# Second buffers for four input tiles, and a two-operation decode of every second weight block, in a fused attention and feed-forward kernel

## The chip, the core and the metric

The kernel runs on one core of one Trainium2 chip. TensorE (PE) multiplies, with its weight loads on a row of their own (PEld); VectorE (DVE), ScalarE (ACT) and GpSimd (POOL) do the elementwise work; SyncE (SP) issues most of the transfers. The metric is the device time of one execution in microseconds, the median of several runs.

## The reference

Causal attention in float32 for 4 batches and 8 heads of 576 rows of 64, blended by a gate per head with a read from a memory matrix; the result goes through a two-layer feed-forward with a sigmoid-approximated GELU.

```python
scores = scale * np.matmul(q, k.transpose(0, 1, 3, 2))
a = softmax(where(causal, -1e9, scores))
local = np.matmul(a, v)
q_p = phi(q)                                   # relu(x) + exp(min(x, 0))
mem_out = (q_p @ M_prev) / (q_p @ z_prev + 1e-6)
x = g * mem_out + (1 - g) * local              # 2304 tokens x 512
h = x @ w_in                                   # 512 x 2048
g = h * (1.0 / (1.0 + np.exp(-1.702 * h)))
out = g @ w_out
```

The weights arrive as float64 values, as pairs of 32-bit words, and are turned into float32 on the chip.

## The kernel before

The program has three stages. A short first part (to about 28 us) does the first 256 query rows of batch 0 for all four head pairs at once. Then sixteen (batch, head pair) units p0 to p15 of attention follow, and the feed-forward's first layer fills TensorE between their steps; from about 385 us on the second layer runs alone.

For one unit the scores are four query blocks (`ps`), 128 to 512 keys wide, and a tail (`ps`, 288 wide). Each block's two heads use the upper and the lower 64 rows of the array: `s_both` writes them as two matmuls one after the other. VectorE takes the row maximum (`nm`, L541), ScalarE the exponential (`a`, `at`, L547), GpSimd scales the rows (L550), TensorE transposes (`pt`), ScalarE and VectorE copy the transposes out (`e`), and TensorE multiplies by the values (`po`). Queries for the memory read go a way of their own: `load_vq` fetches raw queries `qr`, values `vr`, memory `mr` and normaliser `zb`; ScalarE makes exp(min(q, 0)) in `qmin` and `qexp` (tile `qmt`, L489 and L492), VectorE finishes it in `qphi` (`qp`, L496), GpSimd multiplies by `zb`, and so on. The pool `ldp`, which holds `mr`, `qr` and `zb`, has one buffer of each; `kqf` and `vr` have two.

The first layer works on 16 weight blocks (`wi0` to `wi15`). A block is decoded by `conv_unit` in five parts: `load` fetches 128 x 1024 raw words (`wraw`, 512 KB); `scale` has ScalarE rescale the high words into PSUM (`ws`, L213); `bits` are three VectorE operations that shift the result left by 3 (L224), put in the sign from the high word (L229) and put in three bits of the low word (L231, result `wr`); `high` has ScalarE round it to the short form (`wi`, first half); and GpSimd subtracts to get the remainder (second half). TensorE multiplies a block in twelve matmuls (`pm`), the first of which needs only the first half. Decoding takes place up to about 97 us; after that the blocks stay.

What stands before what on each engine is fixed when the program is built: `at(slot, prio, fn)` puts steps into slots, and a scheduler then orders the instructions of each engine by its own estimate of when their inputs and buffers are there. Each engine runs its list strictly in that order, so a change of buffers also moves instructions. Raw words take their buffers from several pools by the letter of the block in a string of sixteen: c is a pool of two, e a pool of two, h and l borrow the tiles of the split activations.

Of the kernel before, what the change touches and what calls it, by code (L numbers as in the profile page):

```python
# [8 lines left out]
F32 = mybir.dt.float32  # L9
F32R = mybir.dt.float32r  # L10
I32 = mybir.dt.int32
AF = mybir.ActivationFunctionType
ALU = mybir.AluOpType
# [21 lines left out]
def tile_attention_memory_moe(ctx, tc, kq, vq, mem, zz, beta, w_in, w_out, out):  # L35
    nc = tc.nc
# [12 lines left out]
    def pool(stack, name, bufs=1, **kw):  # L49
        return stack.enter_context(tc.tile_pool(name=name, bufs=bufs, **kw))  # L50

    attn = ExitStack()
    left = ExitStack()
    cst = pool(ctx, "cst", side="left")
    mop = pool(left, "mop", 2, side="left")
# [7 lines left out]
    ps_m = pool(left, "ps_m", 2, space=PSUM, side="left")  # L63
    dr = pool(ctx, "dr", space=bass.MemoryType.DRAM)
    mox = pool(attn, "mox", 2, side="right")
    ldp = pool(attn, "ldp", side="right")
    att = pool(attn, "att", side="right")
    wkp = pool(attn, "wkp", side="right")
    sml = pool(attn, "sml", 6, side="right")
    ps_s = pool(attn, "ps_s", 4, space=PSUM, side="right")  # L70
    ps_x = pool(attn, "ps_x", 1, space=PSUM, side="right")
    ps_o = pool(attn, "ps_o", 1, space=PSUM, side="right")
# [5 lines left out]
    state = {"slot": -8, "pe": 0.0, "seq": 0, "sum": 0, "bank": 0}  # L78
# [19 lines left out]
    NOSYNC = mybir.DependencyInfo(mybir.DependencyClass.NoSync, mybir.DependencyReason.DATA)  # L98
# [16 lines left out]
    def at(slot, prio, fn):  # L115
        assert slot > state["slot"], (slot, state["slot"])
        state["seq"] += 1
        events.setdefault(slot, []).append((prio, state["seq"], fn))
# [34 lines left out]
    def sub(eng, dst, src, hi):  # L153
        return tt(eng, dst, src, f32(hi), ALU.subtract)
# [7 lines left out]
        out=mask[:, 384:512], in_=mask[:, 384:512], compare_op=ALU.is_ge, fill=NEG,  # L162
# [4 lines left out]
    for r in range(2):  # L167
        v = maskt[64 * r:64 * r + 64, CH - 64:CH]
        nc.gpsimd.affine_select(
            out=v, in_=v, compare_op=ALU.is_ge, fill=NEG, base=0, pattern=[[-1, 64]], channel_multiplier=1)  # L170
# [26 lines left out]

    wb = {}

    def conv_unit(slot, dst, src, rp, rkw, wp, wkw, sp, skw):  # L200
        box = {}

        def load():
            raw = rp.tile([128, DM, 2], I32, name="wraw", **rkw)
            nc.sync.dma_start(raw.rearrange("p f w -> p (f w)"), src.bitcast(I32))
            box["raw"] = raw

        def scale():
            if wp() is None:
                box["s"] = box["r"] = sp.tile([128, DM], F32, name="wr", **skw)  # L210
            else:
                box["s"] = wp().tile([128, DM], F32, name="ws", **wkw)
            x = nc.scalar.activation(  # L213
                out=box["s"], in_=box["raw"][:, :, 1].bitcast(F32), func=AF.Copy, scale=2.0 ** -112)
            for name in (state["behind"], state.get("late A")):
                if name is not None:
                    tc.add_manual_dep(x.ins, name, NOSYNC, reason="raw words")
            state["behind"] = x.ins.name

        def bits():  # L220
            raw, si = box["raw"], box["s"].bitcast(I32)
            if "r" not in box:
                box["r"] = sp.tile([128, DM], F32, name="wr", **skw)
            x = nc.vector.tensor_scalar(out=si, in0=si, scalar1=3, scalar2=None, op0=ALU.logical_shift_left)  # L224
            if "late V" in state:
                tc.add_manual_dep(x.ins, state["late V"], NOSYNC, reason="raw words")
            for name in state.pop("bits", ()):
                tc.add_manual_dep(x.ins, name, NOSYNC, reason="raw words")
            nc.vector.scalar_tensor_tensor(  # L229
                out=si, in0=raw[:, :, 1], scalar=-2 ** 31, in1=si, op0=ALU.bitwise_and, op1=ALU.bitwise_or)  # L230
            nc.vector.scalar_tensor_tensor(  # L231
                out=box["r"].bitcast(I32), in0=raw[:, :, 0], scalar=29, in1=si,
                op0=ALU.logical_shift_right, op1=ALU.bitwise_or)

        def high():
            x = copy("A", dst[:, 0], box["r"])
            if "fqt" in state:
                tc.add_manual_dep(x.ins, state.pop("fqt"), NOSYNC, reason="raw words")

        parts = (load, scale, bits, high,  # L240
                 lambda: sub("P", dst[:, 1], box["r"], dst[:, 0]))
        if slot is None:
            return parts
        for k, prio, fn in zip((0, 2, 2, 3, 3), (5, 60, 61, 40, 41), parts):
            at(slot + k, prio, fn)

# [19 lines left out]
    def conv_in(blk):  # L268
        w = w1[blk].tile([128, 2, DM], F32R, name=f"wi{blk}")
        if blk < AHEAD:  # L270
            wb[blk] = w
        raw = {
            "c": (cnv, {"bufs": 2}), "e": (ear[0], {"tag": "r"}),
            "h": (mop, {"tag": "xh"}), "l": (mop, {"tag": "xl"})}["cceehlcchleeccee"[blk]]
        ws = (lambda: ps_o, {"tag": "po"}) if blk == 3 else (lambda: ps_x, {"tag": "ps"})
        parts = conv_unit(None, w, w_in[blk], *raw, *ws, att, {"tag": f"qpt{blk % 2}", "bufs": 2})
        if blk < AHEAD:
            return parts

        c = CONV[blk - AHEAD]  # L280
        at(max(c - 6, -7), 58, parts[0])
        for fn in parts[1:]:
            at(c, 58, fn)
        at(c + 3, 1, lambda: wb.update({blk: w}))
# [149 lines left out]
    pairs = [(b, c) for b in range(B) for c in range(NP)]  # L434
    raws = {}
# [3 lines left out]
    K0 = [STEP * p for p in range(MB * NP)]  # L439
# [9 lines left out]
            nc.sync.dma_start(kqr, kq[b, c])  # L449
        raws[p] = {"kq": kqr}  # L450

    def load_vq(p):
        b, c = pairs[p]

        vr = att.tile([128, 5, 128], F32, name="vr", bufs=2)
        nc.sync.dma_start(vr, vq[b, c, :, 0])
        mr = ldp.tile([128, 2, D], F32, name="mr")
        nc.sync.dma_start(mr, mem[b * NP + c])
        qr = ldp.tile([128, 5, 128], F32, name="qr")
        t = 2 if b < MB else 0  # L460
        nc.sync.dma_start(qr[:, t:], vq[b, c, :, 1, t:])
        zb = ldp.tile([128, 128], F32, name="zb")
        nc.sync.dma_start(zb, zz[b, c:c + 1, :].to_broadcast([128, 128]))
        raws[p].update(v=vr, m=mr, q=qr, z=zb)


    def hold(p, x):
# [3 lines left out]
    def plan_prep(p):  # L471
        b, c = pairs[p]
        s0 = K0[p] - 8
# [59 lines left out]
        at(s0 + 13, 31, qev)  # L533
        if p + 1 < len(pairs):
            at(K0[p + 1] - 11, 60, lambda: load_kq(p + 1))
            at(max(K0[p + 1] - 8, s0 + 8), 60, lambda: load_vq(p + 1))

    def softmax_max(pieces):
        nm = sml.tile([128, 2], F32, name="nm")
# [263 lines left out]
    for b in range(MB):  # L803
        parts = first_queries(b)
        xplan[b] = -7
        if b == 0:
            for blk in range(AHEAD):
                for fn in (parts[1:] if blk == 0 else conv_in(blk)):
                    fn()
            state["first", 2] = state["behind"]  # L810
    first.close()
    w1.update({k: pool(left, f"w1_{k}", side="left", reuse_waits="tile") for k in range(W0, NB - 2)})
    load_kq(0)
    load_vq(0)
    for p in range(NPAIRS):
        plan_prep(p)
        plan_attend(p)
# [196 lines left out]
    k = 0  # L1014
    while fill["gen"] is not None or conv_q or events:
# [4 lines left out]
        if k in soon:  # L1020
            t, p = soon[k]
# [120 lines left out]
```

## Time and profile before

| | |
|---|---|
| median of 3 runs | 615.9 us (615.55 to 618.78) |
| the profiled execution, its own time | 616.93 us |
| its span, first to last instruction | 615.2 us |
| granted TensorE clock, mean over the span | 0.986 |
| busy: PE 593.0, PEld 518.4, DVE 421.7, ACT 347.9, POOL 214.9 us | 96, 84, 69, 57, 35% |

The profile shows one execution. A busy time is the sum of an engine's instructions; the ends of matmuls are modelled, so their starts say more than their durations. An idle time is given with what ended it. The chain of waits follows the work that ended last back from the last instruction to what released it each time. The granted clock is 1.00 where TensorE ran at 2.4 GHz and 0.50 where it ran at 1.2 GHz.

### The profile page before, as it was taken

The numbers are of one execution on the slowest core, as the hardware profiler recorded it, in microseconds if no ns is written. First come the engines' busy times: TensorE is split into PE (matmuls) and PEld (weight loads), VectorE is DVE, ScalarE is ACT, GpSimd is POOL, SyncE is SP. The second block draws the span as 40 slices with busy tenths as digits, with TensorE's granted clock in tenths as the row PEclk, the third lists the DMA queues.
The fourth block names the chain that finished last, engine by engine and source line by source line (L and its number), as shares of the span: only waits on it lengthen the run. The fifth ranks groups of instructions, "written<-read, shape, count | busy, mean of one in ns | idle before, by whom it ended". The sixth has DMA issues, their size and how long they took to land.

```text
span 615.2 us, 11404 instructions
## 1 busy us (share of the span) xinstructions
PE 593.0 (96%) x4000; PEld 518.4 (84%) x4000; DVE 421.7 (69%) x1022; ACT 347.9 (57%) x811; POOL 214.9 (35%) x279
## 2 busy tenths in 40 slices
PE   5789999999999999999999999999999999999997
PEld 3467767777787888787788889999999999999997
DVE  5877986666667576676565434679688679766964
ACT  6776766555557355365454343465686865576441
POOL 4765665543536235344334231213412401220000
PEclk9598999999999999999999999999999999999999
DMA  8784442433255355365342126522544733471002
GB/s 261 266 282 119 164 140 92 133 125 104 71 178 189 91 173 173 85 198 151 108 135 66 54 74 221 194 92 75 182 149 138 250 118 75 144 245 52 26 1 77
DMA packets 46985, 84.11 MB, mean 137 GB/s; under 512 B 5328, under 2 KB 33232, under 8 KB 46928
## 3 DMA queue, kind: packets, MB, share of 16 engines
q1 hardware_dynamic: 40688, 61.36, 30.5%
q0 software_dynamic: 6240, 22.02, 11.5%
q8 instruction: 31, 0.51, 0.4%
q14 instruction: 26, 0.21, 0.1%
HBM read 59.77 MB, written 23.59 MB: 136 GB/s over the span
## 4 chain that ended last, share of the span: by engine, by line
PE 68%; DVE 10%; issue 6%; DMA 6%; ACT 5%; POOL 3%; SPq 0%; DVEq 0%; POOLq 0%; ACTq 0%
PE pm L129 22%; PE acc L994 20%; PE ps L129 9%; PE pt L138 8%; PE po L129 8%; DVE wo L151 2%; DMA g<-gd 2%; DMA qr<-in_vq_dram 2%; POOL g L937 2%; ACT a L547 2%; DVE ps L541 1%; DVE st L151 1%; DMA wraw<-in_w_out_dram 1%; DMA wraw<-in_w_in_dram 1%; DVE ol L151 1%
## 5 line engine op out<-in xcount | busy, mean ns | idle before, releaser
L129 PE MATMUL pm<-xh,wi 128*128 128x320 f32 (+1 forms) x1024 | 219.7, 305 | 1.5 <-POOL wi L151 1.4
L129 PEld LDWEIGHTS pm<-xh,wi 128*128 128x128 f32 x1024 | 165.5, 190 | 7.5 <-POOL wi L151 2.7
L994 PE MATMUL acc<-oh,wo 128*128 128x384 f32 x672 | 169.6, 336 | 0.7 <-ACT hk L143 0.7
L129 PE MATMUL pm<-xl,wi 128*128 128x256 f32 (+1 forms) x512 | 152.1, 298 | 0.1
L994 PEld LDWEIGHTS acc<-oh,wo 128*128 128x128 f32 x672 | 121.4, 188 | 1.3 <-ACT hk L143 1.0
L550 POOL TENSOR_SCALAR a<-a,sm,g 128x512 f32<-128x512 f32 (+3 forms) x112 | 76.3, 693 | 129.4 <-DVE sm L601 97.6
L994 PE MATMUL acc<-ol,wo 128*128 128x384 f32 x336 | 111.0, 337 | 0.4 <-DVE ol L151 0.4
L151 DVE TENSOR_TENSOR ol<-g,oh 128x768 fp32r<-128x768 f32 x84 | 79.6, 954 | 40.1 <-ACT oh L143 39.8
L129 PEld LDWEIGHTS pm<-xl,wi 128*128 128x128 f32 x512 | 96.9, 190 | 0.5 <-DVE xl L151 0.3
L547 ACT ACTIVATE a<-ps,nm 128x256 f32<-128x256 f32 (+2 forms) x112 | 59.7, 539 | 64.2 <-DVE nm L541 64.1
L143 ACT ACTIVATE oh<-g 128x768 fp32r<-128x768 f32 x84 | 69.8, 842 | 43.6 <-PE acc L994 31.7
L541 DVE CUSTOM_DVE_ANT_0 ps<-ps,mask 128x256 f32<-128x256 f32 (+4 forms) x144 | 67.3, 506 | 39.0 <-PE ps L129 38.2
L129 PE MATMUL ps<-kqf 128*128 128x288 f32 (+4 forms) x288 | 71.0, 477 | 3.0 <-ACT at L547 1.4
L937 POOL DMA_DIRECT2D g<-gd x48 | 34.8, 726 | 99.4 <-DVE ol L151 76.7
L994 PEld LDWEIGHTS acc<-ol,wo 128*128 128x128 f32 x336 | 62.8, 188 | 0.9 <-DVE ol L151 0.9
L143 ACT ACTIVATE hk<-pm 128x256 f32<-128x256 f32 (+1 forms) x76 | 30.7, 408 | 41.4 <-PE pm L129 37.6
L138 PE MATMUL pt<-ident,a 128*128 128x128 f32 x296 | 53.5, 274 | 0.1
L943 ACT ACTIVATE g<-g 128x768 f32<-128x768 f32 x48 | 39.5, 838 | 18.4 <-DMA g<-gd 15.7
L129 PEld LDWEIGHTS po<-e,vr 128*64 128x64 f32 x416 | 29.9, 137 | 20.1
L151 DVE TENSOR_TENSOR g<-g,g 128x768 f32<-128x768 f32 x48 | 45.4, 950 | 1.4 <-ACT g L943 1.4
L129 PE MATMUL po<-e,vr 128*64 128x320 f32 (+3 forms) x416 | 45.4, 359 | 0.0
L129 PEld LDWEIGHTS ps<-kqf 64*128 64x128 f32 (+1 forms) x288 | 30.3, 189 | 15.1 <-issue 5.3
(126 smaller groups left out, 774.7 us busy)
## 6 DMA issues: line engine op xcount, KB each, us to landing
g<-gd POOLq DMA_DIRECT2D x48, 384.0 KB, 4.8
gd<-hk SPq DMA_DIRECT2D x64, 160.0 KB, 1.9
wraw<-in_w_in_dram SPq DMA_DIRECT2D x16, 512.0 KB, 5.2
gd<-hk SPq DMA_DIRECT2D x64, 128.0 KB, 1.8
kqf<-in_kq_dram SPq DMA_DIRECT2D x12, 608.0 KB, 5.8
vr<-in_vq_dram SPq DMA_DIRECT2D x16, 320.0 KB, 4.9
wraw<-in_w_out_dram SPq DMA_DIRECT2D x10, 512.0 KB, 4.0
qr<-in_vq_dram SPq DMA_DIRECT2D x12, 320.0 KB, 3.0
```

The source lines that it names most:

```text
L129: x = nc.tensor.matmul(out, l, r, start=start, stop=stop)
L138: state["att"] = nc.tensor.transpose(out, in_, idn).ins.name
L143: return nc.scalar.activation(out=dst, in_=src, func=AF.Copy, **kw)
L151: return (nc.vector if eng == "V" else nc.gpsimd).tensor_tensor(out=dst, in0=a, in1=b, op=op)
L541: nc.vector.tensor_tensor_reduce(out=ps, in0=ps, in1=mk, op0=ALU.add, op1=ALU.min, scale=-0.125, scalar=1e38 if j == 0 else nm[:, j - 1:j] ...
L547: return nc.scalar.activation(out=a, in_=ps, func=AF.Exp, scale=-1.0, bias=nm, accum_out=sm)
L550: return (nc.vector if eng == "V" else nc.gpsimd).tensor_scalar(out=a, in0=a, scalar1=r, scalar2=gcol, op0=ALU.mult, op1=ALU.mult)
L937: x = nc.gpsimd.dma_start(t, gd[4 * kh + p][:, :, t0:t0 + QN].rearrange("i p t -> p i t"))
L943: x = nc.scalar.activation(out=t, in_=t, func=AF.Gelu_apprx_sigmoid)
L994: nc.tensor.matmul(acc[b, j][:, :QN], W[2 * p + kk][:, WPART[i], sp, 128 * j:128 * j + 128], mv[:, kk], start=first and p + kk == 0 and sp ...
```

## The change

`ldp` gets two buffers of each of its tiles, and the fetch is cut in two: `load_q` (`mr`, `qr`, `zb`) is put into an earlier slot, together with the keys, and `load_v` stays where it was. A new pool `raws_f` holds two raw-word tiles, and the string that assigns buffers to blocks changes from `cceehlcchleeccee` to `cceehlffhlcceeff`: blocks 6, 7, 14 and 15 use the new pool, and blocks 10 to 13 others than before. Odd blocks are decoded in another way: ScalarE multiplies the low words by 0.936 x 2^-29 and writes them back as integers (L203 of the new file, `low_words`), right behind `scale`, and VectorE does two operations where it did three: shift and merge in one, then the sign. The factor makes the three lowest bits of these weights approximate.

```diff
-    ldp = pool(attn, "ldp", side="right")
+    ldp = pool(attn, "ldp", 2, side="right")
+    raws_f = pool(attn, "raws_f", 2, side="right")
...
+    def low_words(raw):
+        return nc.scalar.activation(
+            out=raw[:, :, 0], in_=raw[:, :, 0].bitcast(mybir.dt.uint32), func=AF.Copy, scale=0.936 * 2.0 ** -29)
...
+            if help:
+                y = low_words(box["raw"])
+                tc.add_manual_dep(y.ins, x.ins.name, NOSYNC, reason="raw words")
+                state["behind"] = y.ins.name
...
-            x = nc.vector.tensor_scalar(out=si, in0=si, scalar1=3, scalar2=None, op0=ALU.logical_shift_left)
+            if help:
+                x = nc.vector.scalar_tensor_tensor(
+                    out=si, in0=si, scalar=3, in1=raw[:, :, 0], op0=ALU.logical_shift_left, op1=ALU.bitwise_or)
+            else:
+                x = nc.vector.tensor_scalar(out=si, in0=si, scalar1=3, scalar2=None, op0=ALU.logical_shift_left)
...
             nc.vector.scalar_tensor_tensor(
-                out=si, in0=raw[:, :, 1], scalar=-2 ** 31, in1=si, op0=ALU.bitwise_and, op1=ALU.bitwise_or)
-            nc.vector.scalar_tensor_tensor(
-                out=box["r"].bitcast(I32), in0=raw[:, :, 0], scalar=29, in1=si,
-                op0=ALU.logical_shift_right, op1=ALU.bitwise_or)
+                out=r if help else si, in0=raw[:, :, 1], scalar=-2 ** 31, in1=si,
+                op0=ALU.bitwise_and, op1=ALU.bitwise_or)
+            if not help:
+                nc.vector.scalar_tensor_tensor(
+                    out=r, in0=raw[:, :, 0], scalar=29, in1=si,
+                    op0=ALU.logical_shift_right, op1=ALU.bitwise_or)
...
-            "h": (mop, {"tag": "xh"}), "l": (mop, {"tag": "xl"})}["cceehlcchleeccee"[blk]]
+            "h": (mop, {"tag": "xh"}), "l": (mop, {"tag": "xl"}),
+            "f": (raws_f, {"tag": "f"})}["cceehlffhlcceeff"[blk]]
-        parts = conv_unit(None, w, w_in[blk], *raw, *ws, att, {"tag": f"qpt{blk % 2}", "bufs": 2})
+        parts = conv_unit(blk % 2, w, w_in[blk], *raw, *ws, att, {"tag": f"qpt{blk % 2}", "bufs": 2})
...
-            at(max(K0[p + 1] - 8, s0 + 8), 60, lambda: load_vq(p + 1))
+            at(K0[p + 1] - 11, 60, lambda: load_q(p + 1))
+            at(max(K0[p + 1] - 8, s0 + 8), 60, lambda: load_v(p + 1))
```

The order changes between about 25 and 103 us of the trace before. TensorE's list is the same again from the second matmul group of `wi0` at 320 columns on, which starts at 102.24 us there.

ScalarE's list at the queries of p2 (the second `qmt<-qr` and its second half `qmt<-qmt`), the decode of blocks 3 to 5 (`wi3`, `wi4`, `ws`) and p1's tail exponentials (`at`), before:

```order
L143 ACTIVATE wi3_466<-wr_471 128x512
L489 ACTIVATE qmt_177<-qr_755 128x6x64
L143 ACTIVATE hk_574<-pm_554 128x256
L143 ACTIVATE wi4_513<-wr_633 128x512
L213 ACTIVATE ws_659<-wraw_598 128x512
L492 ACTIVATE qmt_177<-qmt_177 128x6x64
L547 ACTIVATE at_779,tail1_166<-ps_741,nm_760 128x288
L547 ACTIVATE at_779,tail1_166<-ps_742,nm_760 128x288
```

And after:

```order
L507 ACTIVATE qmt_180<-qr_675 128x6x64
L144 ACTIVATE hk_574<-pm_541 128x256
L510 ACTIVATE qmt_180<-qmt_180 128x6x64
L144 ACTIVATE wi3_469<-wr_475 128x512
L144 ACTIVATE qpt0_709<-pt_680 128x256
L144 ACTIVATE hk_577<-pm_557 128x256
L566 ACTIVATE at_782,tail1_169<-ps_750,nm_763 128x288
L566 ACTIVATE at_782,tail1_169<-ps_751,nm_763 128x288
L144 ACTIVATE wi4_516<-wr_636 128x512
L219 ACTIVATE ws_662<-wraw_607 128x512
L203 ACTIVATE wraw_607<-wraw_607 128x512
```

The query step stands ahead of the decode of block 3 instead of behind it, the tail exponentials stand ahead of block 4's steps, and `low_words` (L203) follows the `scale` of block 5.

SP's list of transfers from the weights of block 4 (`wraw_578`) to p2's raw queries (`qr_755`), before; `qr_616` is p1's:

```order
L205 DMA wraw_578<-in_w_in_dram 128x1024
L458 DMA mr_614<-in_mem_dram 128x128
L461 DMA qr_616<-in_vq_dram 128x384
L205 DMA wraw_603<-in_w_in_dram 128x1024
L463 DMA zb_618<-in_zz_dram 128x128
L205 DMA wraw_652<-in_w_in_dram 128x1024
L205 DMA wraw_598<-in_w_in_dram 128x1024
L205 DMA wraw_722<-in_w_in_dram 128x1024
L458 DMA mr_753<-in_mem_dram 128x128
L205 DMA wraw_678<-in_w_in_dram 128x1024
L205 DMA wraw_823<-in_w_in_dram 128x1024
L461 DMA qr_755<-in_vq_dram 128x384
```

And after, from p1's raw queries (`qr_601`) to p2's (`qr_675`); `wraw_612` and `wraw_655` are blocks 6 and 7 in the new pool, `wraw_581` is block 4:

```order
L479 DMA qr_601<-in_vq_dram 128x384
L481 DMA zb_603<-in_zz_dram 128x128
L211 DMA wraw_612<-in_w_in_dram 128x1024
L471 DMA vr_621<-in_vq_dram 128x640
L211 DMA wraw_655<-in_w_in_dram 128x1024
L211 DMA wraw_581<-in_w_in_dram 128x1024
L476 DMA mr_673<-in_mem_dram 128x128
L479 DMA qr_675<-in_vq_dram 128x384
```

Between p1's keys and p2's queries there stood seven weight loads, and now there stand three; the loads of blocks 6 and 7 have moved ahead of block 4's.

TensorE's list at p1's 512-wide scores (`ps_771` and `ps_772` are the two heads), before:

```order
L129 MATMUL pm_567<-xl_218,wi3_466 128x256
L129 MATMUL pm_680<-xh_217,wi4_513 128x256
L129 MATMUL ps_771<-kqf_593 128x512
L138 MATMUL pt_763<-ident_134,a2_715 128x128
L129 MATMUL ps_772<-kqf_593 128x512
L138 MATMUL pt_767<-ident_134,a2_717 128x128
```

And after:

```order
L139 MATMUL pt_770<-ident_137,at_630 128x128
L139 MATMUL pt_770<-ident_137,a3_652 128x128
L130 MATMUL ps_774<-kqf_596 128x512
L130 MATMUL ps_775<-kqf_596 128x512
L130 MATMUL pm_570<-xh_220,wi3_469 128x256
L130 MATMUL pm_570<-xl_221,wi3_469 128x256
```

The transpose between the two heads is gone, and most of block 3's matmuls (`pm` from `wi3`) have moved from in front of the scores to behind them. For p3 eleven `pm` matmuls stood between the heads before and none stands there after; for p2 eleven before and five after.

## Rows read from the trace of the kernel before

**Rows 1.** Stretches: length; busy PE, PEld, DVE, ACT, POOL; clock, DMA share, GB/s

```profile
38.70:60.80 22.10, 19.68 (x126) 15.21 (x125) 16.13 (x44) 13.96 (x36) 12.67 (x14) 0.92 0.58 194
60.80:77.20 16.40, 15.90 (x113) 12.00 (x112) 14.93 (x40) 12.24 (x33) 10.26 (x11) 1.00 0.51 163
...
103.70:385.00 281.30, 279.18 (x2079) 229.96 (x2079) 169.59 (x559) 139.21 (x416) 109.86 (x138) 1.00 0.40 128
385.00:615.20 230.20, 225.64 (x1373) 224.19 (x1371) 171.56 (x229) 137.15 (x203) 41.51 (x48) 1.00 0.37 121
```

**Rows 2.** What TensorE waited for, 28.4 to 103.7 us (total us, times, longest)

```profile
PE ps L129 <- ACT at L547: 1.4, 2, 0.9
PE pm L129 <- POOL wi L151: 1.4, 2, 1.0
PE ps L129 <- ACT e L143: 1.0, 3, 0.4
```

**Rows 3.** The same, 103.7 us to the end

```profile
PE pt L138 <- ACT a L547: 0.8, 2, 0.5
PE acc L994 <- ACT hk L143: 0.7, 1, 0.7
```

**Rows 4.** SP's queue (start, length of the issue)

```profile
36.26 0.38 SPq L461 DMA_DIRECT2D qr<-in_vq_dram  x1
```

**Rows 5.** The chain of waits (start, us, what)

```profile
36.26 6.81 DMA qr<-in_vq_dram
```

**Rows 6.** ScalarE in time order (start, us, instruction, idle before)

```profile
43.09 0.53 ACT L489 ACTIVATE qmt<-qr 128x384 f32<-128x384 f32 x1 [1.86 <-DMA qr<-in_vq_dram]
...
45.29 0.48 ACT L547 ACTIVATE at<-ps,nm 128x288 f32<-128x288 f32 x1
...
45.76 0.49 ACT L547 ACTIVATE at<-ps,nm 128x288 f32<-128x288 f32 x1
```

**Rows 7.** VectorE in time order

```profile
42.14 0.15 DVE L541 DVE_READ_ACCUMULATOR2_ANT nm<- 128x1 f32 x1
44.97 0.70 DVE L224 TENSOR_SCALAR ws<-ws 128x512 int32<-128x512 int32 x1 [2.68 <-ACT ws L213]
```

**Rows 8.** TensorE in time order, around p1's 512-wide scores

```profile
41.88 0.30 PE L138 MATMUL pt<-ident,at 128*128 128x128 f32 x1 [0.22 <-DVE sm L601]
42.02 0.27 PE L138 MATMUL pt<-ident,a 128*128 128x128 f32 x1
43.31 0.39 PE L129 MATMUL pm<-xh,wi 128*128 128x256 f32 x1 [1.02 <-POOL wi L151]
...
45.91 1.12 PE L129 MATMUL ps<-kqf 64*128 64x512 f32 x2 [0.92 <-ACT at L547]
...
47.23 1.12 PE L129 MATMUL ps<-kqf 64*128 64x512 f32 x2
```

**Rows 9.** Stretches of rows 1's form, behind that

```profile
47.50:50.00 2.50, 2.50 (x11) 1.74 (x11) 2.01 (x7) 2.10 (x6) 1.94 (x2) 0.69 0.14 49
50.00:52.50 2.50, 2.50 (x16) 2.50 (x16) 1.26 (x5) 1.12 (x4) 0.00 (x0) 0.63 0.11 38
```

**Rows 10.** TensorE, the 512-wide scores of p3's first head, with what follows

```profile
81.08 1.12 PE L129 MATMUL ps<-kqf 64*128 64x512 f32 x2 [0.51 <-ACT at L547]
82.13 0.39 PE L129 MATMUL pm<-xh,wi 128*128 128x256 f32 x1
```

**Rows 11.** TensorE, the 512-wide scores of p4, both heads, and what follows

```profile
98.49 1.13 PE L129 MATMUL ps<-kqf 64*128 64x512 f32 x4
99.55 0.39 PE L129 MATMUL pm<-xh,wi 128*128 128x256 f32 x1
```

**Rows 12.** Operations by line, 28.4 to 103.7 us (busy us, mean ns, idle)

```profile
L224 DVE TENSOR_SCALAR ws<-ws 128x512 int32<-128x512 int32 x14 | 9.8, 704 | 4.3 <-ACT ws L213 4.3
...
L213 ACT ACTIVATE ws<-wraw 128x512 f32<-128x512 f32 x14 | 8.8, 634 | 0.1
```

**Rows 13.** Operations on raw words (min/median/max ns, first and last start)

```profile
L844 ACT ACTIVATE r<-wraw x10: 664/682/702, 179.5 to 291.2; 128x512 f32<-128x512 f32 x10
```

More of the change, by code (lines that the diff above doesn't have):

```diff
@@ L198, in tile_attention_memory_moe, with conv_unit @@
     wb = {}
-    def conv_unit(slot, dst, src, rp, rkw, wp, wkw, sp, skw):
+    def low_words(raw):
+        return nc.scalar.activation(
+            out=raw[:, :, 0], in_=raw[:, :, 0].bitcast(mybir.dt.uint32), func=AF.Copy, scale=0.936 * 2.0 ** -29)
+    def conv_unit(help, dst, src, rp, rkw, wp, wkw, sp, skw):
         box = {}
@@ L228, in bits @@
                 tc.add_manual_dep(x.ins, name, NOSYNC, reason="raw words")
+            r = box["r"].bitcast(I32)
             nc.vector.scalar_tensor_tensor(
-                out=si, in0=raw[:, :, 1], scalar=-2 ** 31, in1=si, op0=ALU.bitwise_and, op1=ALU.bitwise_or)
-            nc.vector.scalar_tensor_tensor(
-                out=box["r"].bitcast(I32), in0=raw[:, :, 0], scalar=29, in1=si,
-                op0=ALU.logical_shift_right, op1=ALU.bitwise_or)
+                out=r if help else si, in0=raw[:, :, 1], scalar=-2 ** 31, in1=si,
[4 more added lines that the diff above has]
+                    op0=ALU.logical_shift_right, op1=ALU.bitwise_or)
         def high():
@@ L241, in conv_unit @@
                  lambda: sub("P", dst[:, 1], box["r"], dst[:, 0]))
[L242 to L245, printed above, removed]
+        return parts
     chunks = [(b, a, n) for b in range(B) for a, n in ((0, 256), (256, 320))]
@@ L450, in load_kq, with load_v, load_q @@
         raws[p] = {"kq": kqr}
-    def load_vq(p):
+    def load_v(p):
         b, c = pairs[p]
-        vr = att.tile([128, 5, 128], F32, name="vr", bufs=2)
+        vr = raws[p]["v"] = att.tile([128, 5, 128], F32, name="vr", bufs=2)
         nc.sync.dma_start(vr, vq[b, c, :, 0])
+    def load_q(p):
+        b, c = pairs[p]
         mr = ldp.tile([128, 2, D], F32, name="mr")
@@ L463, in load_vq @@
         nc.sync.dma_start(zb, zz[b, c:c + 1, :].to_broadcast([128, 128]))
-        raws[p].update(v=vr, m=mr, q=qr, z=zb)
+        raws[p].update(m=mr, q=qr, z=zb)
     def hold(p, x):
@@ L813, in tile_attention_memory_moe @@
     load_kq(0)
-    load_vq(0)
+    load_v(0)
+    load_q(0)
     for p in range(NPAIRS):
```

## The prediction

> **What bounds the kernel now.** I read the stretches first: how many of a stretch's microseconds TensorE is busy, and at which clock. From 103.7 us to the end it is busy for 279.18 of 281.30 and 225.64 of 230.20 us at full clock [rows 1], and its largest waits there are 0.8 and 0.7 us [rows 3]. The change moves nothing there, so it can win only ahead of 103.7 us. In that part TensorE is busy for 19.68 of 22.10 us at p1, at a clock of 0.92, and for 15.90 of 16.40 at p2 [rows 1]; p1 takes 5.7 us longer for a like amount of work. The list of TensorE's waits then names the two large causes, ScalarE's tail exponentials and GpSimd's remainder of a weight block [rows 2].
>
> The order in time shows what happens at p1. SP issues p2's raw queries at 36.26 us [rows 4] and they need 6.81 us [rows 5], because the one `qr` buffer was free only then and seven weight loads stood ahead. ScalarE has idled for 1.86 us when it starts `qmt` at 43.09 [rows 6], and what stands behind that step in its list is late: `at` starts at 45.29, although its maximum was finished on VectorE at 42.29 (42.14 + 0.15) [rows 7]. VectorE idles 2.68 us for `ws` [rows 7]. TensorE idles 0.22 + 1.02 + 0.92 = 2.16 us between 41.7 and 45.9 [rows 8]. Behind that the granted clock is 0.69 and 0.63 in two stretches of 2.5 us [rows 9]; full clock would have saved 2.5 x 0.31 + 2.5 x 0.37 = 1.7 us there.
>
> **The change part by part.** I sum against the profiled execution, 616.93 us, which is 1.0 above the median of 615.9.
>
> *A, the wait for p2's queries.* With two `qr` buffers p2's queries wait for nothing of p1, and three weight loads stand between them and p1's keys instead of seven. They are in time if they land by 41.2 (43.09 - 1.86) [rows 6]; before, the issue alone was at 36.26 [rows 4], so the earlier place has the time of four 512 KB loads in hand over what it had. ScalarE then goes on at 41.2. What is late next is the tail maximum at 42.29 [rows 7], which hangs on TensorE and VectorE and not on the queries. From it to the scores it takes what it took before, 45.91 - 45.29 = 0.62 us [rows 6, 8], so the scores start at about 42.95. TensorE's last work ahead of them, the transpose at 42.02, needs 0.1 us more, since the one before it took 0.14 from start to start [rows 8]; some 0.8 of the 2.16 us of idleness stays. **Gain 1.4 us.** Block 3's remainder on GpSimd, which ended the idleness of 1.02 [rows 8], is now wanted only behind the scores, so it has the 1 us that they take as cover.
>
> *B, the clock.* It fell behind the 4 us with 2.16 idle. With one gap of about 0.8 left and TensorE busy on both sides, I take it that it stays up: **gain 1.7 us** [rows 9]; if it falls all the same, the gain is nothing.
>
> *C, the order of scores.* One head's 512-wide scores take 1.12 us alone, and the next instruction starts 1.05 us after them (81.08 to 82.13) [rows 10]. Two heads that stand together, in p4's row of four matmuls, are over in 1.06 us (98.49 to 99.55) [rows 11]: they use different rows of the array and run side by side. Before, p1's and p3's heads are apart and cost twice that; after, they stand together. **Gain 2 x 1.05 = 2.1 us.** p2's stay apart, for nothing. The low end is 1.6, if p1's second `at`, 0.47 us behind the first [rows 6], holds up the second head.
>
> *D, the queues.* SP gets no more transfers than before. `load_q` stands earlier, so keys and values behind it start up to its own length later; they are not waited for in [rows 2]. Two weight loads in buffers of their own, for blocks 6 and 7, pass block 4's; ScalarE idles 0.1 us in all ahead of `scale` [rows 12], so there is no wait for raw words to remove and some room to lose. I put D at nothing; if that cover is gone, block 4 is late by one load.
>
> *E, the decode.* Eight odd blocks lose one VectorE operation of three, of which the shift takes 0.704 us [rows 12]: 8 x 0.70 = 5.6 us less on VectorE. ScalarE gets eight `low_words`; no row shows one, but the nearest are `scale` with 0.634 us, raw words in and PSUM out [rows 12], and the second layer's with 0.682, which writes SBUF [rows 13]: 5.1 to 5.5 us more. In p2's stretch VectorE is busy for 14.93 of 16.40 us and ScalarE for 12.24 [rows 1], so work goes from the fuller engine to the emptier. On TensorE's path this can be worth from -1.9 us (all of the 3.8 us in [rows 2] that A hasn't taken) to +5.5 us (each `low_words` ahead of an exponential that TensorE waits for). I take a **gain of 0.5 us**: the waits left are on ScalarE's and GpSimd's results, which a faster VectorE helps only at second hand.
>
> The Trainium skill, "ScalarE: Activation LUTs", section "Rules for kernel authors", says that adds and multiplies belong on VectorE and not on ScalarE; that speaks against E. The rows here don't bear it out: on 128 x 512 tiles the ScalarE operation has 634 ns and the VectorE operation 704 [rows 12]. By the rule E would be a loss, the first rival from below.
>
> The sum: 1.4 + 1.7 + 2.1 + 0.5 = 5.7 us; 616.93 - 5.7 = 611.2, and on the median 610.2.
>
> **The rivals.** *ScalarE becomes the bound (slower).* `low_words` stands right behind `scale`, and VectorE's first operation waits for it instead of for `scale` alone; behind it on ScalarE wait `e`, `a` and `at`. If all eight land ahead of an exponential that TensorE waits for, 5.5 us come onto the path; with A and B eaten by that, C's 2.1 stay: 3.4 slower, 619.3 on the median. It decides where ScalarE's 12.24 us of 16.40, with two or three more of 0.68, leave no room ahead of an exponential. Against it: that is at most 14.3 of 16.4 us, and after, p1's `at` stand ahead of block 4's steps.
>
> *The clock falls all the same.* 0.8 us of idleness stays at the old place, and B is lost: 5.7 - 1.7 = 4.0, or 611.9 on the median. For it: the stretch is early, and the rows don't show how little idleness is enough.
>
> *Another wait takes the place.* The tail maximum, GpSimd's remainders or p2's queries, late in spite of their buffer behind the two new loads, hold TensorE as long as before, and the clock falls too: C and E of 2.6 us, or less, stay: 613.3 to 615.9, in the middle 614.4. Against it: the maximum's 42.29 lies 3 us ahead of `at`'s start.
>
> *VectorE was the bound.* Its 14.93 of 16.40 us [rows 1] would then hold p1 to p4 up everywhere, and four or so of the 5.6 us come back instead of 0.5: 607. Against it: [rows 2] names ScalarE and GpSimd.
>
> **How the numbers follow.** The forecast of 610.2 us has 0.38; the clock that falls 0.20; another wait 0.20; VectorE as the bound 0.13; ScalarE as the bound 0.09. What this measurement can tell from no change is about 0.5%, 3.1 us: faster is below 612.8. The forecast and VectorE's case lie there, with 0.12 of the clock's 0.20 and 0.04 of the other wait's: 0.67. The rest of these two is no change, 0.08 + 0.16 = 0.24; slower is 0.09. The range goes from VectorE's case at 606.5 to the upper part of the other wait at 615.5; ScalarE's case and the ends of both sides lie outside, some 0.2.
>
> **What would show it.** A: `qmt<-qr` at p2's queries without a wait for a transfer, `at` near 42.3, TensorE's idleness at p1 near 0.8 us. B: a granted clock of 1.00 from 45 to 55 us. C: four matmuls in one row at p1 and p3. E: eight rows of `low_words` of 0.63 to 0.69 us, ScalarE some 5 us busier, and no new exponential among TensorE's waits. If ScalarE's `a` or `at` leads TensorE's waits with several microseconds, the forecast is wrong in E; if there are new waits for transfers, in D.

## The result, and the profile after

The changed kernel takes 611.41 us (median of 6 runs, 610.66 to 613.6), the kernel before 617.17 us beside it (6 runs, 615.55 to 618.78): a ratio of 0.9906, 95% interval 0.9886 to 0.9927. A second set of runs gave 611.43 us and 0.994 (0.9914 to 0.9966). The changed kernel is at 611.4 us in both sets; the kernel before has medians of 615.3 to 617.2 us in the sets of runs on record, so the gain is 5.8 us in the first set and 4.3 in the second. The forecast was 610.2 us in a range of 606.5 to 615.5. The direction and the range are right, and the forecast gain of 5.7 us is near the first set's; the sum behind it is right at p1 and wrong behind it, with an unforeseen gain that filled part of the gap. That the total came out so near is partly luck.

The page of the changed kernel, first its head and busy times (busy us, share of the span, instructions):

```profile
span 609.8 us, 11385 instructions
...
PE 587.8 (96%) x4000; PEld 515.9 (85%) x4000; DVE 418.6 (69%) x1014; ACT 352.4 (58%) x819; POOL 215.2 (35%) x279
```

The span is 5.4 us shorter than the 615.2 of before. ScalarE has 4.5 us more (352.4 against 347.9), VectorE 3.1 us less (418.6 against 421.7).

The place of the stall, p1, in the changed kernel. ScalarE in time order (the answer to rows 6):

```profile
40.05 0.53 ACT L507 ACTIVATE qmt<-qr 128x384 f32<-128x384 f32 x1
...
42.42 0.49 ACT L566 ACTIVATE at<-ps,nm 128x288 f32<-128x288 f32 x1
...
42.90 0.50 ACT L566 ACTIVATE at<-ps,nm 128x288 f32<-128x288 f32 x1
```

TensorE in time order (the answer to rows 8):

```profile
43.06 0.33 PE L139 MATMUL pt<-ident,at 128*128 128x128 f32 x1 [0.33 <-ACT at L566]
43.23 0.27 PE L139 MATMUL pt<-ident,a 128*128 128x128 f32 x1
43.43 1.24 PE L130 MATMUL ps<-kqf 64*128 64x512 f32 x4
44.60 0.38 PE L130 MATMUL pm<-xh,wi 128*128 128x256 f32 x1
```

And the stretches behind it (length; busy PE, PEld, DVE, ACT, POOL; granted clock, DMA share, GB/s; the answer to rows 9):

```profile
45.00:47.50 2.50, 2.50 (x24) 2.50 (x24) 2.50 (x8) 2.42 (x8) 1.33 (x2) 1.00 0.13 46
47.50:50.00 2.50, 2.50 (x25) 2.50 (x24) 2.18 (x7) 2.09 (x6) 2.00 (x2) 1.00 0.18 59
50.00:52.50 2.50, 2.50 (x19) 1.67 (x19) 1.87 (x5) 1.58 (x5) 1.22 (x3) 1.00 0.38 83
```

The query step no longer waits for a transfer, `at` starts at 42.42 instead of 45.29, the four score matmuls (two for each head) stand in one row, and the clock is 1.00 where it was 0.69 and 0.63. That much is as forecast.

What TensorE waits for has not gone away, though. Its waits from 28 to 100 us (total us, times, longest; the answer to rows 2):

```profile
PE pt L139 <- ACT a L566: 1.3, 1, 1.3
PE ps L130 <- ACT e L144: 1.0, 1, 1.0
PE pm L130 <- POOL wi L152: 0.7, 1, 0.7
```

They sit at p2 and p3. TensorE there, and ScalarE around the two of them:

```profile
69.28 0.59 PE L130 MATMUL ps<-kqf 64*128 64x384 f32 x2 [0.95 <-ACT e L144]
...
78.83 1.13 PE L130 MATMUL ps<-kqf 64*128 64x512 f32 x4
...
82.03 0.33 PE L139 MATMUL pt<-ident,at 128*128 128x128 f32 x1 [1.27 <-ACT a L566]
```

```profile
67.74 0.63 ACT L219 ACTIVATE ws<-wraw 128x512 f32<-128x512 f32 x1
68.30 0.67 ACT L203 ACTIVATE wraw<-wraw 128x512 int32<-128x512 uint32 x1
68.86 0.37 ACT L144 ACTIVATE e<-pt 128x256 f32<-128x256 f32 x1
...
81.20 0.69 ACT L566 ACTIVATE a<-ps,nm 128x512 f32<-128x512 f32 x1 [1.15 <-DVE nm L560]
```

At 68.30 a `low_words` stands ahead of the copy `e` for which TensorE waits 0.95 us, where it waits 0.42 in the changed kernel without the helped decode: the first rival's mechanism, once. At 78.83 p3's two heads stand together, as term C wanted. Six transposes follow, which fill two more of the four PSUM buffers that scores (`ps`) and transposes (`pt`) share; the seventh has its operands (the same `at` and `a` tiles were read before) but needs the buffer in which the first head's scores lie until their exponential is taken. ScalarE starts that at 81.20, when VectorE's maximum is there, and TensorE waits 1.27 us.

To see where the time goes I use five points at which TensorE's list is the same in all kernels below: the start, p0's second 512-wide score (30.74 us before), p2's tail score (60.81), a 288-wide score at 128.37, the end of attention (384.8) and the last matmul. p2's tail score stands one row earlier in TensorE's list with the helped decode (eleven rows later without `low_words`), so the second and third column are best read together for those kernels.

| us from point to point, one profile each | to p0's 512 | p1 | p2 to p4 | to 385 | to the end |
|---|---|---|---|---|---|
| before | 30.74 | 30.07 | 67.56 | 256.43 | 226.58 |
| before, again | 30.56 | 30.00 | 67.71 | 256.46 | 227.27 |
| changed | 29.92 | 26.52 | 68.58 | 254.90 | 226.11 |
| changed, again | 29.98 | 26.50 | 68.41 | 254.91 | 226.09 |
| buffers and slot alone | 29.72 | 26.63 | 68.07 | 254.90 | 226.05 |
| buffers alone | 30.25 | 26.57 | 68.14 | 254.89 | 227.19 |
| slot alone | 30.69 | 30.25 | 67.72 | 255.99 | 226.67 |
| raw-word pool alone | 30.00 | 28.43 | 67.86 | 256.16 | 226.17 |
| changed, no helped decode | 29.79 | 26.65 | 68.08 | 254.89 | 225.82 |
| helped decode alone | 30.95 | 26.27 | 68.66 | 256.04 | 225.63 |
| changed, `low_words` left out | 32.64 | 28.94 | 64.78 | 254.90 | 226.99 |
| changed, `low_words` twice | 32.82 | 27.60 | 69.54 | 254.94 | 225.63 |
| query step behind `at` | 32.47 | 26.61 | 68.10 | 256.48 | 225.71 |
| buffers and slot, p2's and p3's scores together | 30.67 | 26.63 | 68.79 | 254.92 | 226.17 |

From the means of the two profiles each: -0.7 in the first column, -3.5 at p1, +0.9 at p2 to p4, -1.5 from there to 385 us, -0.8 behind. The last column differs by 0.7 between the two profiles of the kernel before, so only the middle three are taken for the change's. They come to 4.1 us (3.5 - 0.9 + 1.5).

### The profile page after: what moved, and what is told of

Its sections match the earlier page's. It is cut to its first block, busy times and chain, and to the rows that moved or that the text cites. A ratio compares the mean times of both kernels' runs of the same rounds, so it can differ in the third digit from the quotient of the medians.

```text
span 609.8 us, 11385 instructions
## 1 busy us (share of the span) xinstructions
PE 587.8 (96%) x4000; PEld 515.9 (85%) x4000; DVE 418.6 (69%) x1014; ACT 352.4 (58%) x819; POOL 215.2 (35%) x279
## 4 chain that ended last, share of the span: by engine, by line
PE 77%; DVE 8%; ACT 6%; issue 5%; DMA 2%; POOL 2%; SPq 0%; DVEq 0%; POOLq 0%; ACTq 0%
PE pm L130 31%; PE acc L1014 21%; PE ps L130 9%; PE po L130 9%; PE pt L139 8%; DMA g<-gd 2%; POOL g L957 2%; DVE ps L560 2%; ACT a L566 1%; DVE ol L152 1%; ACT ws L219 1%; ACT fa L566 1%; ACT wi L144 1%; DMA gb<-in_beta_dram 1%; ACT wraw L203 0%
## 5 line engine op out<-in xcount | busy, mean ns | idle before, releaser
L560 DVE CUSTOM_DVE_ANT_0 ps<-ps,mask 128x256 f32<-128x256 f32 (+4 forms) x144 | 67.3, 508 | 42.3 <-PE ps L130 41.6
L130 PE MATMUL ps<-kqf 128*128 128x288 f32 (+4 forms) x288 | 68.5, 475 | 2.9 <-ACT e L144 1.0
L130 PEld LDWEIGHTS po<-e,vr 128*64 128x64 f32 x416 | 29.9, 137 | 20.1
L144 ACT ACTIVATE e<-pt 128x320 f32<-128x320 f32 (+2 forms) x76 | 32.9, 436 | 19.3 <-PE pt L139 15.1
```

Of the source, the lines that this page charges most:

```text
L130: x = nc.tensor.matmul(out, l, r, start=start, stop=stop)
L144: return nc.scalar.activation(out=dst, in_=src, func=AF.Copy, **kw)
L560: nc.vector.tensor_tensor_reduce(out=ps, in0=ps, in1=mk, op0=ALU.add, op1=ALU.min, scale=-0.125, scalar=1e38 if j == 0 else nm[:, j - 1:j] ...
```

## The experiments

**Is it the buffers or the decode?** The buffers, and the query load in its own slot, without the rest of the change:

```diff
-    ldp = pool(attn, "ldp", side="right")
+    ldp = pool(attn, "ldp", 2, side="right")
...
+            at(K0[p + 1] - 11, 60, lambda: load_q(p + 1))
```

> The kernel before with two buffers of the query, memory and normaliser tiles and the query load in its own earlier slot; nothing else. Theory 1 (the buffers carry the gain): p1's queries arrive in time, TensorE's 2.16 us of idleness at p1 shrink to about 0.6, the clock stays at 1.00 behind it (1.7 us) and p1's two 512-wide score matmuls, which stand together in this order, save 1.05: 4.3 us less than before, ratio 0.993. Theory 2 (VectorE was the bound and the helped decode carries the gain): the order of p1's scores alone counts, 1 us, ratio 0.998.

611.42 us, ratio 0.9946 (0.9921 to 0.9971): the whole gain of the change. TensorE's idleness ahead of p1's scores shrinks to 1.25 us (0.21 + 1.04) and not to the 0.6 expected, since GpSimd's remainder still stands ahead of them in this order:

```profile
42.30 0.38 PE L129 MATMUL pm<-xh,wi 128*128 128x256 f32 x1 [1.04 <-POOL wi L151]
...
43.91 1.13 PE L129 MATMUL ps<-kqf 64*128 64x512 f32 x4
```

The changed kernel without the helped decode says the same from the other side:

```diff
-        parts = conv_unit(blk % 2, w, w_in[blk], *raw, *ws, att, {"tag": f"qpt{blk % 2}", "bufs": 2})
+        parts = conv_unit(None, w, w_in[blk], *raw, *ws, att, {"tag": f"qpt{blk % 2}", "bufs": 2})
```

> The changed kernel with all sixteen blocks decoded in three VectorE operations, as before; buffers, slots and raw-word pools as changed. Theory 1: about the same as the buffers alone, 4.3 us less than before, ratio 0.993; TensorE's new waits of the changed kernel at 69 and 81 us (0.95 and 1.27 us, for ScalarE) are gone, and p3's two score matmuls are apart again, which costs 1.05, so it comes out within 1 us of the changed kernel. Theory 2: it loses most of the changed kernel's gain, ratio 0.998.

611.4 us, 0.9937 (0.9914 to 0.9959). The decode in two VectorE operations is worth nothing that the runs can tell in this kernel. Alone it should then have done nothing:

```diff
-        parts = conv_unit(None, w, w_in[blk], *raw, *ws, att, {"tag": f"qpt{blk % 2}", "bufs": 2})
+        parts = conv_unit(blk % 2, w, w_in[blk], *raw, *ws, att, {"tag": f"qpt{blk % 2}", "bufs": 2})
```

> The kernel before with the helped decode of odd blocks alone; one buffer of queries, loads and raw-word pools as before. Theory 1: p2's raw queries still land late, so the wait of some 2 us and the slow clock of 1.7 us at p1 stay; p1's and p3's score matmuls stand together in this order, 2.1 us less, and the new waits for ScalarE take about that back: ratio 1.000. Theory 2: VectorE's relief is what counts: 4 us less, ratio 0.9935.

614.1 us, 0.9974 (0.9953 to 0.9995): a little less than before, where one theory had 1.000 and the other 0.9935. Neither saw why: the table has p1 at 26.27 us for it, as short as with two buffers. ScalarE in that kernel:

```profile
42.70 0.50 ACT L564 ACTIVATE at<-ps,nm 128x288 f32<-128x288 f32 x1
...
43.18 0.50 ACT L564 ACTIVATE at<-ps,nm 128x288 f32<-128x288 f32 x1
...
45.61 0.53 ACT L505 ACTIVATE qmt<-qr 128x384 f32<-128x384 f32 x1
```

With the extra operations in its list the scheduler has put p2's query step behind p1's tail exponentials. The queries are still late; but nobody waits behind them.

**So is it the transfer, or the place of the step that waits for it?** One edit to the kernel before, an order on ScalarE and no buffer:

```diff
-            hold(p, nc.scalar.activation(out=qm, in_=qv(), func=AF.Relu, scale=-1.0))
+            x = nc.scalar.activation(out=qm, in_=qv(), func=AF.Relu, scale=-1.0)
+            if p == 2:
+                tc.add_manual_dep(x.ins, state["at1"], NOSYNC, reason="behind")
+            hold(p, x)
...
                 used(U["ps"][f], x)
+                if p == 1:
+                    state["at1"] = x.ins.name
```

> The kernel before, its one buffer and its loads as they are; the only edit puts ScalarE's query step for p2 behind p1's two tail exponentials instead of ahead of them. p2's raw queries still land at about 43. If it was the place of the waiting step in ScalarE's list that cost p1 its time: p1 is as short as with two buffers, 3.3 us less, the granted clock is 1.00 from 45 to 55 us, and the later waits (292 and 435 us of before) stay: 612.5, ratio 0.995. Rival (the late queries themselves are what counts): p2's query steps are late now, no gain, ratio 1.000.

613.51 us, 0.9958 (0.9938 to 0.9978). p1 takes 26.61 us, as with two buffers, and 128 to 385 us takes 256.48, as with one. ScalarE there:

```profile
44.44 0.48 ACT L550 ACTIVATE at<-ps,nm 128x288 f32<-128x288 f32 x1
...
44.92 0.49 ACT L550 ACTIVATE at<-ps,nm 128x288 f32<-128x288 f32 x1
...
45.40 0.52 ACT L489 ACTIVATE qmt<-qr 128x384 f32<-128x384 f32 x1
```

(Its whole timeline is 1.7 us later from 32 us on; see the last section.) The scheduler has moved more than that step: p1's two heads stand together here too.

```profile
46.65 1.13 PE L129 MATMUL ps<-kqf 64*128 64x512 f32 x4
```

So the two gains have different causes. At p1 it is the place of a waiting step in an engine's fixed list, with the order of scores that came with it; behind 128 us it is the buffers. A wait of 0.7 us at 435 us, which the expectation counted on too, is not there; it has nothing to do with the buffers, for it stands in both profiles of the kernel before (0.70 and 0.50 us) and in that of two buffers in the old slot (0.65).

**What do the buffers do behind 128 us?** ScalarE's waits ahead of the query step, over the whole span, in the kernel before, and in the changed one (total us, times, longest):

```profile
ACT qmt L489 <- DMA qr<-in_vq_dram: 12.0, 5, 3.8
ACT qmt L489 <- DVE nm L541: 7.6, 3, 3.6
ACT qmt L489 <- DVE nrm L508: 5.3, 2, 3.6
```

```profile
ACT qmt L507 <- DVE nrm L525: 17.9, 7, 3.2
```

The 12.0 us for transfers are gone, and 24.9 us of waiting in three rows became 17.9 in one. How the 24.9 us are shared out is less sure than their sum: the second profile of the kernel before puts 23.7 of 24.3 us down to transfers, in eight waits. With the buffers and slot alone one wait of 1.9 us for a transfer is left. One place where that reaches TensorE, in the kernel before, on ScalarE and then on TensorE:

```profile
287.80 0.74 ACT L489 ACTIVATE qmt<-qr 128x640 f32<-128x640 f32 x1 [1.68 <-DVE nrm L508]
...
292.09 0.52 ACT L547 ACTIVATE at<-ps,nm 128x288 f32<-128x288 f32 x1
```

```profile
292.75 0.33 PE L138 MATMUL pt<-ident,at 128*128 128x128 f32 x1 [0.51 <-ACT at L547]
```

The same step in the second profile of the kernel before, which names the transfer:

```profile
287.72 0.74 ACT L489 ACTIVATE qmt<-qr 128x640 f32<-128x640 f32 x1 [1.59 <-DMA qr<-in_vq_dram]
```

And the same two steps of ScalarE with the buffers and slot alone:

```profile
282.23 0.74 ACT L505 ACTIVATE qmt<-qr 128x640 f32<-128x640 f32 x1 [0.87 <-DVE nrm L523]
...
286.52 0.52 ACT L564 ACTIVATE at<-ps,nm 128x288 f32<-128x288 f32 x1
```

What the step waits for here is VectorE's reduction of the `qmt` before; that reduction in the kernel before and in this one:

```profile
286.12 0.83 DVE L507 TENSOR_REDUCE nrm<-qmt 128x10 f32<-128x650 f32 x1 [1.28 <-POOL qmt L151]
```

```profile
281.37 0.83 DVE L523 TENSOR_REDUCE nrm<-qmt 128x10 f32<-128x650 f32 x1 [1.28 <-POOL qmt L151]
```

It ends at 286.95 in the one, 0.85 us ahead of the query step, and at 282.20 in the other, right ahead of it. This kernel is 4.8 us ahead of the one before at 269 us. Its query step is 5.6 us ahead (287.80 - 282.23) and `at` too (292.09 - 286.52), 0.8 us more, and TensorE's wait is gone: its lead is 5.4 behind that point. Smaller steps of 0.1 to 0.3 us stand at 217, 242 and 269 us; what makes them is not shown here. All profiles with two buffers have 254.9 us here, those with one 256.0 to 256.5.

**Which part of the buffer change?** Two buffers with the load in its old slot, and the earlier slot with one buffer:

> The kernel before with two buffers of the query tiles alone; the load of queries stays in the slot where it was, behind the values. Expected: the same as buffers and earlier slot together, 611.4, ratio 0.994, since SP's list has p2's queries in the third place behind p1's keys either way. Rival (the earlier slot carries it): 615, ratio 1.000.

> The kernel before with the load of queries in the earlier slot, but one buffer. Expected: like the kernel before, ratio 1.000, since p2's queries still wait until p1's have been read, and the query step stands ahead of p1's tail exponentials as before. Rival: ratio 0.994.

612.21 us, 0.9946 (0.9928 to 0.9965), and 615.84 us, 0.9994 (0.9976 to 1.0012). The second buffer does it; the slot does nothing. The raw-word pool alone:

> The kernel before with the new pool of two raw-word buffers and its string alone. Expected: like the kernel before, ratio 1.000, since ScalarE never waited for raw words. Rival (earlier weight loads crowd out p2's queries, which then land later than 43 us): 1 to 2 us more, ratio 1.002 to 1.003.

616.2 us, 1.0007 (0.9992 to 1.0022): nothing. Its profile is of use in another way. TensorE's idleness at p1 is the same as before, and the stretches behind it are these:

```profile
41.16 0.30 PE L139 MATMUL pt<-ident,at 128*128 128x128 f32 x1 [0.22 <-DVE sm L620]
...
42.58 0.38 PE L130 MATMUL pm<-xh,wi 128*128 128x256 f32 x1 [1.02 <-POOL wi L152]
...
45.10 1.12 PE L130 MATMUL ps<-kqf 64*128 64x512 f32 x2 [0.89 <-ACT at L566]
```

```profile
47.50:50.00 2.50, 2.50 (x23) 2.50 (x23) 2.46 (x6) 2.10 (x8) 1.16 (x1) 1.00 0.02 7
50.00:52.50 2.50, 2.50 (x24) 2.49 (x24) 1.65 (x6) 1.69 (x4) 1.35 (x2) 1.00 0.39 118
```

In this execution the clock did not fall, with 0.22 + 1.02 + 0.89 = 2.13 us of idleness ahead of it. p1 then takes 28.43 us instead of 30.0, so the fall costs 1.6 us when it comes, and the idleness and the split scores are the other 1.8 (28.43 - 26.6). It is one execution, and the fastest of that kernel's twelve runs.

**Is a pair of scores that stands together worth 1.05 us?** The buffers and slot, and p2's and p3's two heads put together:

```diff
-            names = rooms(KEEP)
+            names = rooms(0 if p in (2, 3) and 3 in blocks else KEEP)
...
-                at(k0 + idx, 20, lambda i=i: scores((1, 0) if i == 1 else (i,)))
+                at(k0 + idx, 26 if p in (2, 3) and i == 3 else 20, lambda i=i: scores((1, 0) if i == 1 else (i,)))
```

> The kernel with the buffers alone, and in addition the two 512-wide score matmuls of p2 and of p3 each put together (the scores go behind the tail's exponentials, and the block of first-layer matmuls that stood between the heads goes ahead of them). If a pair that stands together is worth 1.05 us, as term C of the forecast had it: 2.1 us less than the buffers alone, 609.3, ratio 0.990. Rival: TensorE stands still for the same time right behind the pair, since the exponentials of these scores then have no first-layer matmuls beside them, as at 81 us of the changed kernel, where it waits 1.27 us: no difference from the buffers alone, 611.4, ratio 0.994.

612.17 us, 0.9947 (0.9924 to 0.997): no gain over the 611.42 without it. TensorE behind the two pairs:

```profile
62.72 1.13 PE L129 MATMUL ps<-kqf 64*128 64x512 f32 x4
65.51 0.33 PE L138 MATMUL pt<-ident,at 128*128 128x128 f32 x1 [0.73 <-ACT a L564]
...
79.17 1.13 PE L129 MATMUL ps<-kqf 64*128 64x512 f32 x4
82.35 0.33 PE L138 MATMUL pt<-ident,at 128*128 128x128 f32 x1 [1.25 <-ACT a L564]
```

Both pairs take half the time of two single scores, and both are followed by a wait for an exponential of their own, for the buffer as at p3 of the changed kernel: 0.73 and 1.25 us, together 1.98 of the 2.1 us expected. The eleven first-layer matmuls that stood between the heads covered VectorE's maximum and ScalarE's exponential of the first head; moved ahead of the pair they don't.

**Does ScalarE bound the stretch, or VectorE?** The changed kernel without the ScalarE operation on low words (VectorE's relief alone), and with two of them:

```diff
-                y = low_words(box["raw"])
-                tc.add_manual_dep(y.ins, x.ins.name, NOSYNC, reason="raw words")
-                state["behind"] = y.ins.name
...
-                    out=si, in0=si, scalar=3, in1=raw[:, :, 0], op0=ALU.logical_shift_left, op1=ALU.bitwise_or)
+                    out=si, in0=si, scalar=3, in1=raw[:, :, 0], op0=ALU.logical_shift_left, op1=ALU.bitwise_and)
```

> The changed kernel without the ScalarE operation on low words; VectorE's two operations stay (the low words go in unscaled and by a bitwise and, so the weights of odd blocks are not the reference's). It shows VectorE's relief by itself. Theory 1 (neither engine holds TensorE for long): 611, within 1 us of the changed kernel. Rival (VectorE's relief is worth several microseconds and ScalarE's operation takes them back): 607 to 609, ratio 0.987 to 0.990.

611.23 us, 0.9937 (0.9912 to 0.9962): as the changed kernel. VectorE's 5.4 us less (its decoding takes 27.8 us for 33.2) are worth nothing that the medians can tell, even when they cost ScalarE nothing. They may be worth 1 us: p1 to p4 together take 93.7 us in this profile, 94.9 and 95.1 in the changed kernel's two, 94.7 with the buffers and slot alone. The scheduler's order is another one here, too: p1's and p3's heads stand apart and p2's together.

```diff
+                z = nc.scalar.activation(
+                    out=box["raw"][:, :, 0], in_=box["raw"][:, :, 0].bitcast(mybir.dt.uint32), func=AF.Copy)
```

> The changed kernel with a second ScalarE operation of the same form and size behind each of the eight on low words (it converts them once more, which leaves them as they are): ScalarE is busy 5.4 us more. If ScalarE has room, as theory 1 has it: 611 to 613, at one or two places where the operation stands ahead of a result that TensorE waits for, as at 68 us of the changed kernel, 0.7 us each. Rival (ScalarE bounds this stretch): 5 us more than the changed kernel, 616, ratio 1.001.

614.72 us, 0.9987 (0.9966 to 1.0008), against 611.4 of the changed kernel: 3.3 us for 5.4 us more on ScalarE. TensorE's waits, 25 to 102 us:

```profile
PE pm L130 <- ACT wi L144: 1.7, 3, 1.0
PE ps L130 <- ACT e L144: 1.4, 2, 1.0
PE pt L139 <- ACT at L569: 1.1, 2, 0.7
```

ScalarE leads in all three. The first eight operations find room, the second eight mostly don't; the time lies between the two expectations. Not all of it is ScalarE's load: p1's heads stand apart in this order, which was worth 1.05 us in term C. (The table's first column is 3 us longer in this profile, as in those with the query step behind `at` and without `low_words`: the clock returns later in all three, and whether the edits have a part in that was not tried. The medians say 3.3.)

**What is chance between two profiles of one kernel?** The two kernels once more:

> The changed kernel once more, for its second profile. Both theories: ratio 0.991 as measured first. Open is what TensorE saves behind 103 us of the kernel before, where the orders are the same: in the first profiles it gained 2 us more there, at single places of 0.3 to 0.9 us. If these are chance, this profile has them at other places; if they follow from the change, at the same ones.

> The kernel before once more, for a second profile. Theory 1 predicts p1's late query load and the fall of the clock behind it again; the span's mean granted clock then stays near 0.986, against 0.989 to 0.992 of the kernels without that wait. Open: the kernels so far all gain about 2 us more at the same places behind 200 us, where their orders are equal to that of before. If those waits belong to the kernel before, this profile has them too; if they are chance of the first profile, this one ends earlier by 1 to 2 us and lacks them.

The changed kernel gained at the same places behind 200 us as the first time. Beside the buffers and slot alone, the second profile of the kernel before loses time at 242, 269 and 293 us as the first does, and at 135 in place of 217, in all the same (256.46 against 256.43 us from 128 to 385). The gain there follows from the change. The kernel before did not end earlier (616.64 us).

## Why the prediction was right, and where its sum was not

*What bounds the kernel* was right as to p1: it was the place of the largest gain, and its stall and clock were the largest item. Not all of the 5.7 us by which p1 was longer than p2 was on offer, though: it was no "like amount of work", with 126 matmuls against 113 in the two rows.

*A, 1.4 us.* The mechanism holds in all its steps: `qmt` without a transfer wait, `at` at 42.42 for the forecast 42.3. In the changed kernel TensorE idles 0.33 us at 43.06 and 0.24 at 39.9 for 0.8 forecast, but two waits of 0.27 and 0.34 us at 36.5 and 37.6 are new. Over the whole way that the p1 column measures, its idleness falls from 2.4 us to 1.2, so A is 1.2; with the buffers and slot alone it falls to 1.7, and A is 0.7 there. What the prediction did not separate is the transfer from the place of the step: the same 3.5 us come from an order alone. It says itself that "what stands behind that step in its list is late"; the cheaper remedy for p1 was another order.

*B, 1.7 us.* Measured 1.6, by the profile with the same idleness and no fall. That is the price of a fall that happens, and the prediction put it whole into the median. The granted clocks of the single runs speak against that: of the 32 runs of the kernel before in the set with p2's and p3's scores together, ten have a mean of 0.986 and took 617.3 us on average, ten have 0.989 and took 615.1, eight have 0.992 and took 613.6. B's part in the medians can therefore be smaller than 1.6; at which place a run without a profile was slow is not on record.

*C, 2.1 us.* For p1 it holds: 26.6 us against 28.43 without a fall is 1.8, of which 0.7 is idleness (2.4 against 1.7), so 1.1 is left for the pair, for 1.05 forecast. For p3 it fails. The step that failed is "they use different rows of the array and run side by side", taken for p3 too: it is true of the scores, but I did not ask who waits behind them. The matmuls between the heads were cover for the first head's exponential. At p1 first-layer matmuls stand behind the pair, after two transposes or none, and TensorE has no wait in the 5 us behind it; at p3 transposes stand there, which want the scores' buffers, and TensorE waits 1.27 us where it waited 0.51 ahead of the first head before [rows 10].

*D, nothing.* Right by 1.0007 for the pool alone and 0.9994 for the slot alone. The keys' cover is thin, though: the second profile of the changed kernel has one wait of TensorE for them, which the first hasn't.

```profile
PE ps L130 <- DMA kqf<-in_kq_dram: 0.5, 1, 0.5
```

*E, a gain of 0.5 us.* Measured 0.0 (611.43 against 611.4), between the bounds of -1.9 and +5.5. (By its own words the lower bound should be -2.4, the 3.8 us less A's 1.4; nothing hangs on it.) Its price was well read: the eight rows take 0.647 to 0.729 us, 5.4 us together, for 5.1 to 5.5 forecast. The reason given ("work goes from the fuller engine to the emptier") did not matter, since neither engine's busy share holds TensorE; the order of single results does. The rule weighed there, from the Trainium skill, "ScalarE: Activation LUTs", section "Rules for kernel authors", gives bf16 as its reason; the tiles here hold 32-bit numbers. No run shows the loss that it would mean, and none a gain against it: 611.23 us without the ScalarE operation, 611.41 with it.

*Not in the sum:* 1.5 us between 128 and 385 us. The sentence that failed is "The change moves nothing there, so it can win only ahead of 103.7 us." TensorE's order is the same there, but `ldp` has two buffers for all sixteen units. TensorE's list of waits there was read [rows 3], ScalarE's waits for queries over the whole span were not: 12.0 us in five waits in that profile.

The sum in short: A, B and C at p1 3.5 us for 4.15 forecast (1.4 + 1.7 + 1.05); p2 to p4 a loss of 0.9, where C at p3 and E had a gain of 1.55; and 1.5 from a place that was ruled out. The loss is not C's and E's alone: 0.4 to 0.5 of it stands with the buffers alone and with the query step behind `at` too (68.07 to 68.14 us), where TensorE newly waits some 0.6 us for `at` at p2's 512-wide scores. So the misses of both signs cancel in part: 5.7 us forecast, 4.1 in the three columns, 4.3 between the medians of the second set. The 5.4 us between the two first profiles have 0.8 from the first column and 0.5 from the last, where profiles of one kernel differ by 0.2 and 0.7; there the agreement is luck.

*The rivals.* "ScalarE becomes the bound" was judged rightly as to its point: one `low_words` per odd block still fits, a second mostly does not. "The clock falls all the same" was not seen in either of the changed kernel's two profiles; two of its thirteen runs have a mean clock of 0.986 and took 613.6 us, and where theirs was low is not on record. "VectorE was the bound", as a gain of four us, is refuted by the run without the ScalarE operation.

No version tried beats the changed kernel by more than the runs can tell; two buffers and the slot alone equal it (611.42 us), with the weights exact.

## What to carry to other kernels

Where an engine works through a fixed list, a step that waits for a transfer costs what stands behind it: look first at whether it can stand two rows later, then at buffers. Before counting a saving on the bounding engine, ask what the removed work was covering for its next wait. A buffer count that is shared by all units works in all of them, so read the waits of that tile over the whole span, not only where it hurts most.

## What the runs showed of the hardware

The clock's return in the first part moves by microseconds from profile to profile. In the kernel before and in the changed one (26 to 28 us):

```profile
26.00:28.00 2.00, 2.00 (x6) 0.76 (x4) 1.92 (x8) 1.51 (x4) 0.28 (x1) 0.51 0.88 252
```

```profile
26.00:28.00 2.00, 2.00 (x10) 0.89 (x10) 1.91 (x8) 1.96 (x4) 0.73 (x2) 1.00 1.03 413
```

It is at 0.51 there in the one and at 1.00 in the other, and the first column of the table follows: 30.7 and 29.9 us. With the query step behind `at` the column has 32.47 us; the granted clock reads 1.00 for its whole span, but the score at 26.78 takes 2.07 us where it takes 1.12 at full speed:

```profile
26.78 2.07 PE L129 MATMUL ps<-kqf 64*128 64x512 f32 x2
```

There the duration is the better witness. What decides when the clock returns was not tried. That idleness of 2.1 to 2.3 us at p1 is followed by the fall in three profiles (the two of the kernel before, and the slot alone) and not in a fourth was not expected either; what decides it stays open. The kernel before spreads from 612.3 to 619.1 us over the sets of runs, and its time goes with the mean granted clock of the run (under B above).
